# Tiles 0 and 1 multiply w_in in float32, and all steps stand in another order

## The chip, the cores and the metric

The kernel runs on one NeuronCore of one Trainium2 chip. The metric is the device time of one execution in microseconds, from start to end of the program on that core. Its engines work side by side, each through its own queue of instructions in program order: PE (TensorE, matmuls, with PEld for the weight loads that run beside them), DVE (VectorE), ACT (ScalarE), POOL (GpSimd) and SP, whose queue here issues every DMA.

## The reference

Three layers follow one another on an input of 2 x 768 rows. Cut to what matters:

```
# 1. attention: 8 heads of 64, in chunks of 32 queries
k_full = [8 memory keys, 16 keys before, the chunk's 32, 8 after]
a = softmax(q_c @ k_full.T / 8);   x = a @ v_full        # x: (2, 768, 512)

# 2. a gated layer with a product over the rows of the sequence
h = gelu_tanh(x @ w_in)                                  # w_in: 512 x 1024
u, v = h[..., :512], h[..., 512:]
v_n = (v - mean(v)) / sqrt(var(v) + 1e-6) * g_ln
gated = u * (w_sg @ v_n + b_sg)                          # w_sg: 768 x 768
x = x + gated @ w_out                                    # w_out: 512 x 512

# 3. a gated layer with a convolution of width 3 along the sequence
h = relu(x @ w_in2)                                      # 512 x 1024
out = (h * sigmoid(conv3(h, conv_w))) @ w_out2           # 1024 x 512
```

The weights w_in, w_out, w_in2, w_out2 and conv_w reach the kernel as 64-bit floats.

## The kernel before, in words

**Tiles.** The 1536 rows are 12 tiles of 128 (0 to 5 are batch 0, 6 to 11 batch 1). Layers 2 and 3 also work in four groups of 384 columns (three tiles each).

**Products in halves.** Outside attention, each operand of a product is scaled by a power of two and split into two float16 halves, hi and lo. `mm3` (line 230) makes a product from three float16 matmuls: hi·hi, hi·lo, lo·hi. This needs work before the first matmul. A weight piece is narrowed from 64 to 32 bits (`cn`, three DVE instructions, lines 251 to 254), its largest magnitude is taken (`ca`, ACT, line 239; `wta`, `wtb`, `wtc`, `wtd` bring it across the partitions over PE, DVE, PE, DVE), then the halves are made (`wh`, ACT, line 281; `wl`, DVE, line 289). A tile's x goes the same way: `xa`, `ta`, `tb`, `tc`, `td`, then `xh` and `xl`. The scale is taken out in the step that reads the result, with a factor that `iv` computes.

**Steps of a tile.** Attention of tile i: loads `lq` (queries and keys) and `lv` (values), scores `qk` on PE, maximum `mx` and difference `sb` on DVE, `ex` on ACT, transposes `pp` on PE, copy `pt` on ACT, `pv` on PE, `rd` and `xn` on DVE. Then x is transposed (`px`, PE) and copied into the float32 tile `xf` (`xc`, ACT). Then `v.i.k` (four steps, one for each 128 rows of w_in, 512 columns each) and `u.i.j` (four steps of 128 output columns, all four k inside) form the two parts of x @ w_in, `vg` and `ug` apply gelu on ACT, and `vb`, `nr`, `np`, `nn`, `vn`, `vh`, `vl` normalize v and halve it.

**Later stages.** `m.g.j.n` is the product with w_sg, `o` the one with w_out, `i` the one with w_in2, `p` the one with w_out2. Between them stand steps of DVE and ACT and, for each group, a scale chain as above (`ga` to `gd`, `ya` to `yd`, `za` to `zd`). `pe` copies results out of PSUM and `st` stores them.

**Order.** The string `ORDER` (line 42) lists all steps in one sequence, and `run` (line 794) emits each in turn. Each engine works through its own part of that sequence in order. Waits between engines come from data and from reuse of buffers alone. A name after `@` is the PSUM slot (M0 to M3 of one bank, D0 and D1 of two) or the row buffer (R0 to R2) that a step opens. The slot's earlier user must have been read out first.

**Fillers.** `W.n` (`warm`, line 222) is n matmuls of zeros with 512 columns. They compute nothing. `ORDER` holds 74 of them, in the steps `W.12`, `W.7`, `W.6`, `W.19`, `W.4`, `W.11`, `W.3`, `W.12`, all of them before `pv.2`.

**Loads.** All DMAs stand in the SP queue, in the order of the string. It begins `lq.0 lq.2 lq.1 lv.2 lv.1 lv.0`, then the four pieces of the v half of w_in (`lw.v.0` and so on), then `lq.5 lq.3 lq.4`, `lw.u.0 lw.u.1`. A load into a buffer that is still read waits on the queue, and what stands behind it waits too: three buffers each for `lq` and `lv`.

Of the kernel before, what the change touches and what calls it, by code (L numbers as in the profile page):

```python
# [44 lines left out]
ta.1 lq.6 wtd.v ca.u.0 mx.3 lg wh.v.0 iv.v.0 sb.3 wh.v.1 wl.v.0 W.11@M0 qk.5@D1 lc ex.3 wl.v.1 wh.v.3 xl.0 W.3@M0
pp.3@M1 wh.v.2 mx.5 ls.2 v.0.0@M0 pt.3 tb.1 sb.5 tc.1 v.0.1 td.1 ex.5 wl.v.3 qk.4@D1 xh.1 lq.8 iv.v.1 pv.3@D0 wl.v.2
mx.4 lq.7 xl.1 sb.4 cn.u.3 ex.4 W.12@M1 pv.2@D1 lv.6 pp.4@M3 lv.5 rd.3 ca.u.3 rd.2 pp.5@M2 xn.3 pt.4 v.0.2 xn.2 xa.3
cn.u.1 px.3@M1 pt.5 xa.2 ta.3 px.2@M3 xc.3 tb.3 ta.2 cn.u.2 ca.s.1 tc.3 v.0.3 v.1.0@M2 xc.2 v.1.1 td.3 tb.2 ca.s.0  # L50
iv.v.3 cwn tc.2 pv.4@D0 td.2 v.1.2 iv.v.2 lv.7 rd.4 xh.3 qk.6@D1 lw.o.1 xn.4 lw.o.2 v.1.3 xh.2 xl.3 lq.9 px.4@M1
# [825 lines left out]
```

## Time and profile before

| | us |
|---|---|
| median of 3 runs (347.4 to 348.97) | 347.87 |
| the profiled execution, its own time | 348.18 |
| span of its trace, first to last instruction | 346.4 |
| PE busy in that span | 326.9 (94%) |
| DVE busy | 250.0 (72%) |
| ACT busy | 216.7 (63%) |
| mean granted clock of TensorE | 0.995 |

The trace is read by stages: the share of busy time of an engine is a mean over stages with different limits. Times within the trace are microseconds from the start of its span. The clock is a fraction of full speed. PE counts as busy also while it multiplies zeros.

### The profile page before, as it was taken

The page shows a single profiled execution, that of the slowest core. Times are in us where ns is not written, and L with a number is a line of the kernel's source. Part 1 is how long each engine was busy: PE and PEld are TensorE (multiplying, and loading weights), DVE is VectorE, ACT ScalarE, POOL GpSimd, SP SyncE. Part 2 cuts the span into 40 slices and gives each one's busy share as a digit, 9 for nine tenths or more (in the row PEclk, how much of TensorE's full clock was granted, in tenths as well). Part 3 has the DMA queues.
Part 4 walks back from the last instruction along what each step waited for, and adds up shares of the span by engine and source line. Part 5 has one row for each costly group of instructions (what it writes and reads, how often), then busy time and mean ns, then how long its engine had stood idle before and what let it go on. Part 6 is the DMA issues. An engine that isn't in the chain of part 4 may idle for free.

```text
span 346.4 us, 8509 instructions
## 1 busy us (share of the span) xinstructions
PE 326.9 (94%) x3638; PEld 196.3 (57%) x3638; DVE 250.0 (72%) x517; ACT 216.7 (63%) x431; POOL 6.6 (2%) x37
## 2 busy tenths in 40 slices
PE   8679798899999899999999999999999999999995
PEld 3435454498766566666676676565555554444442
DVE  2659797999838999999597759997999953670000
ACT  1428398887725959674367738995899735661112
POOL 1000000101000000010010000000000000000000
PEclk9989999999999999999999999999999999999999
DMA  7999949404502450033330000100000001001113
GB/s 292 382 417 406 348 107 339 154 2 131 180 0 65 129 177 5 0 125 123 121 123 2 0 2 1 62 1 0 2 0 2 0 0 63 0 30 62 50 40 122
DMA packets 11909, 35.20 MB, mean 102 GB/s; under 512 B 1760, under 2 KB 1760, under 8 KB 11872
## 3 DMA queue, kind: packets, MB, share of 16 engines
q1 hardware_dynamic: 11872, 34.67, 28.1%
q8 instruction: 28, 0.46, 0.6%
q14 instruction: 9, 0.07, 0.1%
HBM read 31.52 MB, written 3.15 MB: 100 GB/s over the span
## 4 chain that ended last, share of the span: by engine, by line
PE 78%; DVE 9%; ACT 7%; issue 3%; DMA 2%; ACTq 0%; SPq 0%; DVEq 0%
PE up L235 9%; PE warm L226 6%; PE vp L235 4%; PE e0.2_3983 L235 3%; PE e1.2_4078 L235 3%; PE po L477 2%; PE sc L438 2%; DMA raw<-in_w_out_dram 2%; PE o20.2_3975 L235 2%; PE o21.1_4215 L235 1%; PE o21.3_4074 L235 1%; PE o21.0_4084 L235 1%; PE o20.0_3778 L235 1%; PE o21.2_4158 L235 1%; ACT hb L732 1%
## 5 line engine op out<-in xcount | busy, mean ns | idle before, releaser
L235 PEld LDWEIGHTS <-i 128*128 128x128 f16 x384 | 37.1, 98 | 27.0 <-issue 2.2
L235 PEld LDWEIGHTS <-gsp 128*128 128x128 f16 x288 | 28.1, 98 | 32.9 <-issue 0.6
L740 DVE SCALAR_TENSOR_TENSOR cb<-hb,cw,cb 128x768 f32<-128x768 f32 x32 | 32.1, 1012 | 7.7 <-ACT cb L737 7.5
L235 PEld LDWEIGHTS <-vs 128*128 128x128 f16 x288 | 27.4, 98 | 17.5 <-issue 0.8
L235 PE MATMUL up<-xs,win 128*128 128x128 f16 x576 | 36.4, 219 | 0.0
L235 PE MATMUL vp<-win,xs 128*128 128x512 f16 x144 | 36.0, 379 | 0.4 <-DVE scwu L269 0.2
L235 PEld LDWEIGHTS <-win 128*128 128x128 f16 x576 | 33.7, 98 | 4.0 <-DVE win L289 0.2
L235 PEld LDWEIGHTS <-wo 128*128 128x128 f16 x192 | 18.5, 98 | 12.6 <-issue 0.9
L226 PE MATMUL warm<-zero 128*128 128x512 f16 x74 | 21.3, 443 | 1.2 <-DVE zero L202 1.2
L235 PEld LDWEIGHTS <-xs 128*128 128x128 f16 x144 | 13.1, 97 | 14.6 <-issue 3.5
L748 DVE TENSOR_TENSOR gate<-hb,cb 128x768 f32<-128x768 f32 x16 | 15.2, 954 | 4.4 <-ACT cb L745 4.4
L745 ACT ACTIVATE cb<-cb 128x768 f32<-128x768 f32 x16 | 13.4, 840 | 7.1 <-DVE cb L740 6.9
L289 DVE SCALAR_TENSOR_TENSOR gsp<-gate,scz,gsp 128x768 f16<-128x768 f32 x16 | 15.7, 1012 | 2.3 <-ACT gsp L281 2.2
L458 ACT ACTIVATE sring<-sring 128x512 f32<-128x512 f32 x12 | 7.5, 628 | 14.9 <-DVE sring L454 14.7
L281 ACT ACTIVATE gsp<-gate,scz 128x768 f16<-128x768 f32 x16 | 14.2, 930 | 3.0 <-DVE gate L748 1.6
L450 DVE TENSOR_REDUCE mx<-sc 128x8 f32<-128x512 f32 x12 | 8.1, 684 | 9.8 <-PE sc L438 9.8
L737 ACT ACTIVATE cb<-hb,cw 128x768 f32<-128x768 f32 x16 | 14.8, 929 | 0.1
L477 PE MATMUL po<-vw,ptr 64*32 64x65 f32 x768 | 10.6, 225 | 4.3 <-issue 3.9
L239 ACT ACTIVATE gs<-uf 128x384 f16<-128x384 f32 x16 | 8.3, 517 | 10.0 <-DVE uf L635 10.0
L226 PEld LDWEIGHTS <-zero 128*128 128x128 f16 x74 | 7.6, 110 | 11.4 <-issue 5.0
L239 ACT ACTIVATE x2s<-xf 128x384 f16<-128x384 f32 x16 | 8.3, 518 | 8.6 <-DVE xf L676 8.6
L477 PEld LDWEIGHTS po<-vw,ptr 64*32 64x32 f32 x768 | 8.5, 105 | 8.1 <-issue 5.7
(403 smaller groups left out, 686.1 us busy)
## 6 DMA issues: line engine op xcount, KB each, us to landing
qk<-in_qk_dram SPq DMA_DIRECT2D x12, 624.0 KB, 6.2
vw<-in_vw_dram SPq DMA_DIRECT2D x12, 520.0 KB, 6.8
raw<-in_w_out_dram SPq DMA_DIRECT2D x12, 512.0 KB, 3.5
raw<-in_w_in_dram SPq DMA_DIRECT2D x8, 512.0 KB, 3.5
ts<-in_w_sgt_dram SPq DMA_DIRECT2D x3, 768.0 KB, 11.0
...
```

The source lines that it names most:

```text
L226: self.nc.tensor.matmul(ps, self.zero[:, :P], self.zero, start=True, stop=True)
L235: self.nc.tensor.matmul(ps, a, b, start=first and i == 0, stop=last and i == n - 1)
L239: self.nc.scalar.activation(room, src, AF.Abs, scale=2.0 ** (1 - EXP_TOP), accum_out=acc)
L281: self.nc.scalar.activation(hi, src, AF.Copy, scale=sc[:, 0:1])
L289: self.nc.vector.scalar_tensor_tensor(out=lo, in0=src, scalar=sc[:, 0:1], in1=hi, op0=ALU.mult, op1=ALU.subtract)
L450: self.nc.vector.tensor_reduce(out=m, in_=self.scv(i), axis=AX.X, op=ALU.max)
L458: self.nc.scalar.activation(self.s(i), self.s(i), AF.Exp, scale=0.125)
L477: self.nc.tensor.matmul(po[c * CH:(c + 1) * CH, par, hp * (D + 1):(hp + 1) * (D + 1)], t[rows, hp, c * CH:(c + 1) * CH], v[rows, c, hp, :] ...
L737: self.nc.scalar.activation(self.c(f), self.h(f)[:, 1:S + 1], AF.Copy, scale=self.cw[:, f, 1:2])
L740: self.nc.vector.scalar_tensor_tensor(out=self.c(f), in0=self.h(f)[:, 2 * side:S + 2 * side], scalar=self.cw[:, f, 2 * side:2 * side + 1], ...
L745: self.nc.scalar.activation(self.c(f), self.c(f), AF.Sigmoid)
L748: self.nc.vector.tensor_tensor(out=self.gate(b, f), in0=self.h(f)[:, 1:S + 1], in1=self.c(f), op=ALU.mult)
```

## The change

It does four things.

1. For tiles 0 and 1 (`PLAIN`), `v.i.k` becomes one float32 matmul of 512 columns, of `xf` with the narrowed float32 piece of w_in, in place of three float16 ones. `u.i.j` becomes four float32 matmuls of 128 columns in place of twelve.
2. For these two tiles the steps `xa`, `ta`, `tb`, `tc`, `td`, `xh`, `xl`, `iv.v` and `iv.u` are gone, and gelu reads the result with a factor of 1.
3. The fillers go from 74 to 38: `W.0.8`, `W.1.16`, `W.3.5`, `W.2.3`, `W.4.3`, `W.5.3` (the first number is a name, the second the count).
4. All other steps stay the same in kind and number, but the whole string, with the loads in it, is in another order. The loads now begin `lw.v.0 lq.0 lw.v.2 lw.v.3 lq.1 lw.v.1 lv.0`.

The start of the new string, up to the first steps of tile 4, and the edits of the code:

```diff
+PLAIN = (0, 1)
+lw.v.0 lq.0 lw.v.2 lw.v.3 lq.1 lw.v.1 cn.v.0 ca.v.0 lv.0 W.0.8@M0 qk.0@D0 mx.0 W.1.16@M1 cn.v.2 ca.v.2 sb.0 qk.1@D1
+lw.u.0 lv.1 lq.2 lw.u.1 W.3.5@M2 ex.0 cn.v.3 ca.v.3 lw.u.2 pp.0@M3 lq.3 pt.0 lv.2 W.2.3@M0 pv.0@D0 lq.4 cn.v.1
+ca.v.1 ls.1 wta.v@M1 W.4.3@M2 mx.1 sb.1 rd.0 xn.0 px.0@M3 xc.0 wtb.v wtc.v W.5.3@M0 ex.1 v.0.0@M2 wtd.v wh.v.0
+wh.v.2 cn.u.0 ca.u.0 cn.u.1 pp.1@M1 pt.1 wh.v.1 wl.v.0 ca.u.1 v.0.1 v.0.2 pv.1@D1 wh.v.3 wl.v.2 rd.1 xn.1 qk.2@D0
+v.0.3 qk.3@D1 mx.2 sb.2 ls.0 px.1@M3 vg.0@R0 lw.u.3 lg ex.2 mx.3 qk.4@D0 wl.v.1 xc.1 pp.2@M0 lv.3 sb.3 lb cn.u.2
+lv.4 lc lq.5 v.1.0@M1 ex.3 pp.3@M2 mx.4 sb.4 pt.2 pv.2@D1 rd.2 xn.2 ca.s.1 v.1.1 v.1.2 ex.4 pp.4@M3 pt.3 xa.2 ca.u.2
+cn.u.3 pv.3@D0 rd.3 ta.2 tb.2 pt.4 px.2@M0 u.1.0@M2 lw.o.0 tc.2 xn.3 ca.u.3 wl.v.3 ls.2 wta.u@M3 wtb.u xc.2 v.1.3
+lv.6 wtc.u lq.6 xa.3 ta.3 td.2 iv.v.2 xh.2 u.1.1 lv.5 ca.s.0 wtd.u wh.u.2 tb.3 vb.0 wh.u.1 tc.3 xl.2 td.3 pv.4@D1
+rd.4 cwn px.3@M0 xc.3 u.1.2 qk.5@D0 lq.8 lw.o.2 v.2.0@M3 ca.s.2 xn.4 px.4@M0 xc.4 v.2.1 wl.u.1 xh.3 u.1.3 lq.7
+wta.s@M0 mx.5 sb.5 wl.u.2 v.2.2 wtb.s wtc.s xl.3 wtd.s iv.v.3 wh.u.3 xa.4 lw.o.1 qk.6@D0 wl.u.3 v.2.3 iv.u.2 ta.4
+tb.4 mx.6 ex.5 ug.1 v.3.0@M0 v.3.1 sb.6 tc.4 td.4 v.3.2 wh.u.0 wl.u.0 pp.5@M2 vg.1@R1 vb.1 xh.4 pt.5 lv.7 v.3.3
+vg.2@R2 wh.s.0 u.2.0@M1 qk.7@D0 pv.5@D1 xl.4 v.4.0@M2 vb.2 rd.5 xn.5 iv.v.4 u.2.1 wh.s.5 wh.s.1 nr.0 np.0 v.4.1 xa.5
...
     def v(self, i, k):
         b, ts = self.ts(i)
+        if i in PLAIN:
+            self.nc.tensor.matmul(self.bank(f"vp{i}"), self.xf(b)[:, k, ts], self.f32("v", k)[:, 0],
+                                  start=k == 0, stop=k == KD - 1)
+            return
...
     def u(self, i, j):
         b, ts = self.ts(i)
+        if i in PLAIN:
+            for k in range(KD):
+                self.nc.tensor.matmul(self.bank(f"up{i}")[:, j * P:(j + 1) * P],
+                                      self.f32("u", k)[:, 0, j * P:(j + 1) * P], self.xf(b)[:, k, ts],
+                                      start=k == 0, stop=k == KD - 1)
+            return
...
     def vg(self, i):
-        self.nc.scalar.activation(self.v_(i), self.bank(f"vp{i}"), AF.Gelu_apprx_tanh, scale=self.inv(f"x{i}", "v"))
+        self.nc.scalar.activation(self.v_(i), self.bank(f"vp{i}"), AF.Gelu_apprx_tanh, scale=self.inv(f"x{i}", "v") if i not in PLAIN else 1.0)
```

`ug` takes the same edit as `vg`, and `warm` a second argument for its name. In the new string the four `u.0` steps come later, among those of tile 3.

## Rows read from the trace of the kernel before

**Rows 1.** Stretches: length; PE, PEld, DVE, ACT, POOL busy us; clock; DMA share; GB/s.

```profile
0.00:70.00 70.00, 58.02 (x1179) 32.06 (x1180) 50.16 (x129) 40.95 (x80) 2.92 (x30) 0.98 0.82 302
70.00:340.00 270.00, 266.48 (x2452) 163.35 (x2451) 199.81 (x389) 174.14 (x347) 3.73 (x7) 1.00 0.15 49
```

**Rows 2.** The same view in other stretches, of the first 40 us and of 33.5 to 64.2.

```profile
0.00:10.00 10.00, 8.81 (x211) 4.23 (x211) 2.78 (x5) 2.25 (x3) 1.70 (x29) 1.00 0.82 308
10.00:20.00 10.00, 5.11 (x155) 3.53 (x149) 6.04 (x12) 4.00 (x9) 0.00 (x0) 0.98 1.01 385
20.00:30.00 10.00, 9.62 (x105) 4.72 (x104) 6.76 (x17) 4.28 (x12) 0.00 (x0) 0.85 1.03 411
30.00:40.00 10.00, 8.12 (x221) 4.63 (x220) 8.37 (x19) 5.48 (x10) 0.00 (x0) 1.00 1.04 383
...
33.50:64.20 30.70, 25.43 (x614) 15.04 (x612) 25.41 (x70) 22.59 (x45) 0.23 (x1) 1.00 0.70 242
```

**Rows 3.** The chain that ended last: start us, length us, what it stood on.

```profile
15.37 3.92 issue
19.61 5.87 PE warm L226 x19
...
81.86 1.34 PE up L235 x24
```

**Rows 4.** Timeline: start us, us, engine, line, operation; brackets: idle before, what ended it.

```profile
6.19 1.32 PEld L438 LDWEIGHTS sc<-qk 64*32 64x32 f32 x128 [0.61 <-DMA qk<-in_qk_dram]
...
14.15 0.43 DVE L251 TENSOR_SCALAR tv<-rawv 128x512 int32<-128x512 int32 x1 [2.61 <-DMA rawv<-in_w_in_dram]
...
19.12 0.43 DVE L251 TENSOR_SCALAR tv<-rawv 128x512 int32<-128x512 int32 x1 [0.99 <-DMA rawv<-in_w_in_dram]
...
27.59 0.60 PE L527 MATMUL px<-ident,xx 128*128 128x128 f32 x4
...
33.48 0.81 PE L235 MATMUL vp<-win,xs 128*128 128x512 f16 x3
...
64.21 0.81 PE L235 MATMUL vp<-win,xs 128*128 128x512 f16 x3
```

**Rows 5.** Groups by line and shape, PE: busy us, mean ns of one, idle before.

```profile
L226 PE MATMUL warm<-zero 128*128 128x512 f16 x74 | 21.3, 443 | 1.2 <-DVE zero L202 1.2
L235 PEld LDWEIGHTS <-xs 128*128 128x128 f16 x144 | 13.1, 97 | 14.6 <-issue 3.5 <-DVE xs L289 0.2
L477 PE MATMUL po<-vw,ptr 64*32 64x65 f32 x768 | 10.6, 225 | 4.3 <-issue 3.9 <-ACT ptr L470 0.2
L438 PE MATMUL sc<-qk 64*32 64x64 f32 x768 | 10.3, 224 | 2.0 <-issue 1.8
L527 PE MATMUL px<-ident,xx 128*128 128x128 f32 x48 | 7.3, 277 | 0.9 <-DVE scwo L269 0.8
L527 PEld LDWEIGHTS px<-ident,xx 128*128 128x128 f32 x48 | 5.5, 141 | 2.6 <-ACT ptr L470 1.0 <-PE warm L226 0.6 <-ACT xf L531 0.2
```

**Rows 6.** The same view, DVE: steps that are removed, and those ahead of the first product.

```profile
L289 DVE SCALAR_TENSOR_TENSOR xs<-xf,scx,xs 128x512 f16<-128x512 f32 x12 | 8.7, 742 | 0.0
L450 DVE TENSOR_REDUCE mx<-sc 128x8 f32<-128x512 f32 x12 | 8.1, 684 | 9.8 <-PE sc L438 9.8
L254 DVE SCALAR_TENSOR_TENSOR tv<-rawv,tv 128x512 int32<-128x512 int32 x4 | 2.8, 692 | 0.1
L251 DVE TENSOR_SCALAR tv<-rawv 128x512 int32<-128x512 int32 x4 | 1.7, 423 | 3.6 <-DMA rawv<-in_w_in_dram 3.6
```

**Rows 7.** The same view, ACT: table loads and the steps that are removed.

```profile
L281 ACT ACTIVATE xs<-xf,scx 128x512 f16<-128x512 f32 x12 | 8.4, 714 | 0.4 <-DVE scx L269 0.4
L239 ACT ACTIVATE xs<-xx 128x512 f16<-128x512 f32 x12 | 7.6, 630 | 2.1 <-DVE xx L496 2.1
L458 ACT ACT_TABLE_LOAD x3 | 3.8, 1283 | 0.8 <-PEq L866 0.7
```

**Rows 8.** A wait of the SP queue: waiting line, waited for, total us, times, longest us.

```profile
SPq L300 <- PE po L477: 38.3, 7, 22.5
```

More of the change, by code (lines that the diff above doesn't have):

```diff
@@ L47 @@
[L47 to L51, printed above, removed]
@@ new lines @@
+o.1.0.0@M0 xl.7 o.1.2.1 td.8 iv.v.8 pv.10@D0 o.1.0.1 os.1.2 o.1.1.0@M1 gl.0.0 o.0.1.0@M2 iv.u.8 os.1.0 oa.1.0
+o.1.1.1 oa.1.2 gl.0.1 o.0.1.1 iv.v.7 rd.9 xn.9 xa.9 o.1.3.0@M0 os.1.1 oa.1.1 o.0.0.0@M1 rd.10 xn.10 xa.10 os.0.1
+o.1.3.1 o.0.0.1 ta.9 oa.0.1 os.1.3 tb.9 o.0.2.0@M2 xh.8 xl.8 vb.6 o.0.3.0@M0 os.0.0 oa.0.0 o.0.2.1 os.0.2 ta.10
+oa.1.3 o.0.3.1 px.9@M1 oa.0.2 ya.1@M2 os.0.3 tc.9 u.6.2 tb.10 tc.10 xc.9 td.9 iv.u.9 xh.9 px.10@M0 oa.0.3 xc.10 yb.1
+yc.1 yd.1 yh.1.1 yh.1.0 td.10 xh.10 iv.v.10 v.7.0@M1 xl.9 qk.11@D1 ya.0@M2 yb.0 v.8.0@M0 yc.0 yd.0 mx.11 sb.11 v.7.1
@@ new lines @@
+v.11.0@M0 ca.i0.1 v.10.2 v.11.1 vl.6 wta.i0@M1 v.10.3 wtb.i0 wtc.i0 vg.9@R2 vl.8 vg.10@R0 u.11.0@M2 wtd.i0 yi.i0.1
+yi.i0.0 wh.i0.3 wh.i0.0 wh.i0.1 wh.i0.2 v.11.2 m.2.1.0@M1 vb.9 u.11.1 m.3.0.0@M3 v.11.3 vg.11@R1 vb.10 wl.i0.1
+wl.i0.0 i.0.3.0.0@D1 i.0.0.0.0@D0 lw.i1.0 cn.i1.0 lw.i1.3 ca.i1.0 wl.i0.2 vb.11 nr.3 np.3 m.2.0.0@M0 wl.i0.3
+i.0.0.1.0 i.0.0.0.1 hr.0.0.0 nn.3 vn.9 vh.9 i.0.3.1.0 cn.i1.3 i.0.0.1.1 vl.9 u.11.2 vn.10 vn.11 lw.p0.2 m.2.0.1
+hr.0.0.1 i.0.1.0.0@D0 hc.0.0 ca.i1.1 iv.u.11 cn.i1.2 u.11.3 vh.10 i.0.1.1.0 cn.p0.0 i.0.1.0.1 i.0.1.1.1 vh.11 vl.11
@@ new lines @@
+lw.p1.2 ca.p0.0 mg.3.0 ma.3.0 m.3.1.2 i.0.5.0.0@D1 ms.3.2@R1 mg.3.2 ms.2.3@R2 ms.3.1@R0 ca.p0.3 i.0.2.1.1 hg.0.3
+hm.0.3 wh.i1.2 i.0.5.1.0 ca.p0.1 yi.i1.0 m.3.3.1 mg.2.3 ma.2.3 wl.i1.2 cn.p1.2 i.0.5.1.1 i.0.5.0.1 hr.0.2.1 m.3.3.2
+ga.2@M0 hr.0.5.1 cn.p1.0 lw.p1.3 hr.0.5.0 hc.0.5 i.0.4.0.0@D1 cn.p1.1 gb.2 ca.p0.2 mg.3.1 ma.3.2 i.0.2.0.1 gc.2
+i.0.4.1.0 i.0.4.0.1 ca.p1.0 hr.0.2.0 hc.0.2 gd.2 gh.2.0 gh.2.1 i.0.6.0.0@D0 ms.3.3@R1 ma.3.1 hs.0.5.0 i.0.4.1.1
+i.0.6.1.0 hs.0.5.1 mg.3.3 ma.3.3 gl.2.0 o.2.1.0@M1 hg.0.5 hs.0.2.0 hs.0.2.1 ga.3@M2 o.2.2.0@M0 o.2.0.0@M3 gb.3
@@ new lines @@
+p.0.2.0@M3 p.0.0.0@M1 p.0.3.0@M0 hs.1.1.1 wh.p1.2 wh.p0.1 hg.1.1 hs.1.2.0 hs.1.2.1 zh.0.1 zl.0.1 i.1.4.1.0 i.1.4.0.1
+hm.1.1 wh.p1.1 wl.p1.1 hg.1.2 i.1.4.1.1 hr.1.3.0 hr.1.3.1 p.0.0.1 p.0.1.0@M2 p.0.4.0@D1 p.0.2.1 p.0.5.0 hm.1.2
+hr.1.4.0 hr.1.4.1 i.1.5.0.0@D0 zh.0.3 zl.0.3 zh.0.4 zl.0.4 p.0.5.1 zh.0.2 zl.0.2 hc.1.3 zh.0.6 zl.0.6 p.0.1.1
+wh.p1.3 wh.p0.2 wh.p0.3 p.0.4.1 wl.p0.1 i.1.5.1.0 wl.p1.2 wl.p0.2 p.0.3.1 i.1.5.1.1 p.0.4.2 zh.0.7 p.0.0.2 hs.1.3.0
+hs.1.3.1 p.0.3.2 hc.1.4 wl.p1.3 zl.0.7 p.0.4.3 p.0.3.3 p.0.5.2 p.0.4.4 i.1.5.0.1 p.0.5.3 p.0.4.5 p.0.3.4 hg.1.3
@@ L121 @@
+p.1.2.4 p.1.3.4 p.1.2.5 p.1.3.5 p.1.2.6 pe.1.1@R0 st.1.1 p.1.3.6 p.1.2.7 pe.1.2@R2 st.1.2 p.1.3.7 pe.1.3@R1 st.1.3
 """
@@ L220, in consts, with warm @@
             nc.gpsimd.memset(self.red[n], 2.0 ** -120)
-    def warm(self, n):
-        ps = self.ps.tile([P, 512], F32, tag=self.slot, name="warm")
+    def warm(self, i, n):
+        ps = self.ps.tile([P, 512], F32, tag=self.slot, name=f"warm{i}")
         for _ in range(n):
```

119 lines of the change are left out of this document (45 added, 74 removed).

## The prediction

> **What bounds the kernel now.** I read the stretches of the span first. After 70 us PE is busy for 266.5 of 270 us [rows 1], and at full rate: 24 matmuls of 128 columns take 1.34 us [rows 3], 56 ns each. There only fewer matmuls would help. In the first 70 us PE is busy for 58.0, but 21.3 of these are the 74 fillers [rows 5], all issued before the first product of tile 1. Real work in the first 70 us is 36.7; 33.3 us are idle or zeros. That is what a better start could win, at most.
>
> Next the chain that ended last, in that stretch: it stands on fillers and on a wait of 3.92 us [rows 3]. So PE waits for something. The timeline says for what: the first scores start when a DMA lands at 6.19, DVE begins to narrow w_in at 14.15, again behind a DMA, and the first product starts at 33.48 [rows 4]. Up to 40 us the DMAs move 383 to 411 GB/s once they run [rows 2]. Before the first product stand three tiles of attention on the load queue and, on DVE, ACT and PE, the scales and halves of w_in and x. From 33.5 to 64.2 PE and DVE are both 83% busy and ACT 74% [rows 2]: a region in which the engines wait on one another, and which prepares u, w_sg and the later tiles.
>
> **The change, part by part.**
>
> *Float32 products.* The nearest rows are the transposes px: four of 128 float32 columns end in 0.60 us [rows 4], and one alone lasts 277 ns [rows 5], so they follow each other every (600-277)/3 = 108 ns, against 56 for float16. Scores and pv, which are float32 matmuls, show 768 instructions for 12 x 32 calls [rows 5], so a float32 matmul is two instructions. Per 128 columns that makes 2 x 108 = 216 ns, against 3 x 56 = 168 for the three float16 ones. v: 8 matmuls of four such widths, 6.9 us for 5.2. u: 32 matmuls, 6.9 for 5.4. Sum +3.2 us of PE. Upper bound: a float32 load of 128 columns lasts 141 ns against 97 [rows 5]; if all 80 stood open, 11.3 us more, so +14.5. The lower bound is the 108 ns once per matmul, -3.6, which the two instructions speak against. I take +3.2: px runs at its rate with the same loads hidden.
>
> The Trainium skill ("TensorE: Matmul & The Clock Gate", section "Weight-path perf modes — Fast Weight Load (FWL) and DoubleRow") says that the fast weight load is off for FP32, which speaks against this change. The 141 against 97 ns agree in direction, though whether loads then stand in the open no row here shows for a real float32 product. By its figure for a plain load, an estimate of 107 ns for 128 columns, all 80 in the open would make +11.8 instead of +3.2 us.
>
> *What leaves.* For two tiles, xl (0.74) and the small tb, td and iv on DVE, 1.5 us and somewhat over; xh (0.71) and xa (0.63) on ACT, 2.7 us [rows 6, 7]; ta and tc, a few tenths of PE. All of it counts only in the start, where these engines set the pace. Against it, the new string switches ACT between exp and gelu more often: counted from both strings, 13 table loads for 11, +2.6 us at 1.28 [rows 7]. They lie on ACT in the stretch that matters, and I carry them there.
>
> *Loads.* What moves earlier or later is DMA issue in SP's queue too. Bytes from the shapes: lq 0.64 MB, lv 0.53, a piece of w_in 0.52. Now 1.28 MB are in at 6.2 us, 4.04 at 14.15, 5.61 at 19.1 [rows 4]. The same line through the new order gives lq.0 (1.16 MB) at 6, lw.v.1 (3.37) at 12.2, lv.0 (3.9) at 13.8, lw.u.3 (10.55) at 31, lv.4 (12.0) at 35. The last two at 0.4 MB per us [rows 2].
>
> *The first product.* DVE narrows three pieces and does mx.0 and sb.0 while loads arrive. After lw.v.1 at 12.2 it still has cn.v.1 (0.42 + 2 x 0.69 = 1.8), mx.1 and sb.1 (0.68 each), rd.0 and xn.0 (1.0): done at 16.4 [rows 6]. px (0.6) and xc (0.6) with their hand-overs put v.0.0 at 18, instead of 33.5: 15 us earlier. The fillers fall from 74 to 38, but they only ever filled.
>
> *From there to the first step of tile 4.* I compare the stretch from v.0.0 to the first product of tile 5 now (33.5 to 64.2) with xn.0 to v.4.0 after. Steps counted from the strings, each at its mean: DVE 28.8 us now, 33.3 after (eight wl for two, ten mx and sb for five, four cn for five, three xl for five); ACT 25.6 now, 34.7 after (nine wh for none, two more ex, a ug, three table loads for one). Now 28.8 and 25.6 show as 25.4 and 22.6 busy [rows 2], a factor of 0.88, so 29.4 and 30.6 after. At the 83% that the fuller engine reaches now, DVE needs 35.4 us from 16.4, ACT 36.9 from 17.9: v.4.0 starts between 51.8 and 54.8. I take 53.3.
>
> *The end.* Real PE work now: 326.9 busy less 21.3 = 305.6; after, 308.8. Done before v.5.0 at 64.2 now: nine qk at 0.86, six pv at 0.88, seven pp and six px at 0.6, sixteen v at 0.65 and small ones [rows 4, 5], together 32.0; left 273.6. The span has 346.4 - 64.2 = 282.2 us for it, so 8.6 are idle (the stores of the end among them). Done before v.4.0 after: eight qk, six pv, six pp, five px, 6.9 of float32 v, 3.5 of float32 u, eight v, one u, small ones: 35.6; left 273.2. With the same 8.6 idle the span is 53.3 + 273.2 + 8.6 = 335.1. The profiled execution lies 1.8 above its span and 0.3 above the median: 336.6, say **336.5 us**.
>
> Later stages I leave as they are. Summed along the strings in the same way, the work that stands ahead of m.0.2.2 is now 79 us on DVE and 59 on PE, after the change 76 and 67; ahead of i.0.0.0.0 it is 148 and 127 now, 142 and 145 after. DVE has less of a lag to make up, so PE should run full there. The tightest place is the last third of m, where m.0.2.2 waits for vl.4, which stands behind mx.10 on DVE, which waits for qk.10 on PE.
>
> **The rivals.**
>
> *More is won (326 to 331).* If DVE and ACT run at 97% in the start instead of 83%, v.4.0 starts at 16.4 + 30.3 to 17.9 + 31.5, about 48, and the time is 331; with the later idle halved, 327. For it: the new order has more steps ready at a time. Against: no stretch of the start shows both engines so full.
>
> *Part is given back (341.5 to 346).* Open weight loads cost up to 11.3 us, of which u.0 and the late half lie where PE is the bound: 5 to 6 more. Or a load is late: SP takes its steps in order, and now has waited 22.5 us behind one pv [rows 8]. In the new string lq.7 stands behind lq.8, which waits for qk.5; its 17.5 MB are in at about 49, and qk.7 is due at 51. Each us beyond stands in front of v.4.0. Either gives 342 to 346.
>
> *No change (346.1 to 349.6).* Both together, about 11 us, and the end is where it was.
>
> *Slower (350 to 365).* The clock. After the idle of 3.92 us the granted clock of 20 to 30 us is 0.85 [rows 2, 3], so part of it ran at 1.2 GHz, while fillers covered the rest of the start. With half the fillers, small gaps could hold PE at 1.2 GHz from 18 to 53 us. PE's 32 us of work there would need up to 64, so v.4.0 would come up to 29 us late. The point from which it is a loss: 14 us late, a mean clock of about 0.65 in that stretch. Against: from 30 to 40 us PE had gaps of 19% at 1.00 [rows 2].
>
> The Trainium skill (the same page, section "Part 1: The HAM clock gate (the "warmup" mystery)") says that the slow clock is the default and activity lifts it, so fewer fillers speak for this rival. The drop to 0.85 behind the idle stretch agrees.
>
> **How the numbers follow.** Forecast, 331 to 341: 0.52. More won: 0.13. Part given back, 341 to 346.1: 0.18. No change: 0.07. Slower: 0.10. A measurement of this kernel tells about 0.5% from no change, 346.1 to 349.6. Faster is then 0.83, same 0.07, slower 0.10. The range from 327 to 346.5 leaves out slower, most of no change and the edge below.
>
> **What the profile will show.** If the steps are right: first float32 product at 17 to 20 us; v.4.0 at 52 to 55; 0.86 us for each float32 v or u step; fillers about 11 us; clock above 0.95 in every stretch from 10 us on; PE over 98% busy from 60 us on. I am wrong if v.4.0 is in time and PE idles over 9 us behind it, if PE's real work exceeds 312 us, or if the clock stays low after 20 us.

## The result, and the profile after

| | before | after |
|---|---|---|
| median, us | 347.63 (347.37 to 348.97) | 335.83 (333.63 to 337.3) |
| ratio, 95% interval | | 0.965 (0.959 to 0.971) |
| profiled execution, us | 348.18 | 336.14 |
| span, us | 346.4 | 334.3 |
| PE busy, us | 326.9 | 319.8 |
| fillers, us (count) | 21.3 (74) | 11.9 (38) |
| DVE, ACT busy, us | 250.0, 216.7 | 250.5, 215.7 |
| mean granted clock | 0.995 | 0.995 |

The kernel is 11.8 us faster, and 335.83 stands 0.7 us beside the forecast of 336.5. One execution among all runs, of e2 (350.44 us), was in a slower state of the chip and is left out of its median. The stretches of the changed kernel come first; columns as in [rows 1] and [rows 2], and the last line is of the kernel before.

```profile
0.00:70.00 70.00, 62.00 (x1296) 42.20 (x1297) 54.30 (x127) 48.79 (x84) 3.18 (x30) 0.98 0.79 284
70.00:334.30 264.30, 257.76 (x2266) 154.10 (x2263) 196.24 (x379) 166.94 (x344) 3.94 (x7) 1.00 0.17 58
...
0.00:10.00 10.00, 6.16 (x76) 2.57 (x77) 3.38 (x7) 2.01 (x3) 1.70 (x29) 1.00 0.80 249
20.00:30.00 10.00, 7.31 (x235) 4.24 (x235) 9.72 (x18) 9.24 (x16) 0.00 (x0) 1.00 1.03 403
30.00:40.00 10.00, 9.80 (x199) 6.83 (x199) 6.22 (x14) 6.71 (x14) 0.00 (x0) 0.83 0.90 324
...
19.76:55.94 36.18, 32.58 (x834) 22.42 (x834) 29.71 (x73) 31.57 (x55) 0.00 (x0) 0.95 0.92 335
55.94:334.30 278.36, 271.82 (x2490) 166.61 (x2484) 209.19 (x409) 178.35 (x361) 5.42 (x8) 1.00 0.17 59
```
```profile
70.00:346.40 276.40, 268.87 (x2462) 164.23 (x2460) 199.81 (x389) 175.79 (x351) 3.73 (x7) 1.00 0.15 51
```

The first two lines answer to [rows 1], and they hold the whole balance. All fillers lie in the first 70 us, so PE's real work there is 62.0 - 11.9 = 50.1 us, where it was 36.7: 13.4 more. Real work in the whole span is 319.8 - 11.9 = 307.9, where it was 305.6: 2.3 more. Behind 70 us 6.5 are idle (264.3 - 257.8) for 7.5 before (276.4 - 268.9). 13.4 - 2.3 + 1.0 = 12.1, which is the difference of the spans. The gain was made in the start and nowhere given back.

The chain that ended last, pieces of the start (start us, length us, what it stood on):

```profile
3.25 10.79 DMA rawv<-in_w_in_dram
...
19.76 1.13 PE vp L547 x2
...
27.35 2.85 issue
...
31.68 1.71 PE vp L547 x2
...
38.92 0.89 PE up L558 x8
...
39.95 0.86 PE vp L547 x2
...
46.88 7.46 DMA qk<-in_qk_dram
...
57.44 0.65 PE vp L236 x3
...
58.52 0.67 PE up L236 x12
```

Read from the top: the last piece of w_in's v half lands at 14.04, the first product stands at 19.76 (33.48 in [rows 4]). A float32 step of v takes 0.86 us and one of u 0.89, against 0.65 and 0.67 for the steps in halves lower down. v.1.0 at 31.68 takes 1.71, twice as long, in the stretch with the clock at 0.83. Ahead of it stands a piece of 2.85 us named "issue", of which more below. v.4.0 follows at 55.94. Just ahead of it PE waits once more, for the load lq.7:

```profile
54.47 0.85 PE L439 MATMUL sc<-qk 64*32 64x64 f32 x64 [0.71 <-DMA qk<-in_qk_dram]
```

The groups by line and shape that answer to [rows 5] (busy us, mean ns of one, idle before):

```profile
L547 PE MATMUL vp<-tv,xf 128*128 128x512 f32 x16 | 9.0, 670 | 0.0
L558 PE MATMUL up<-xf,tu 128*128 128x128 f32 x64 | 8.7, 278 | 0.0
...
L558 PEld LDWEIGHTS up<-xf,tu 128*128 128x128 f32 x64 | 7.9, 192 | 0.4
L547 PEld LDWEIGHTS vp<-tv,xf 128*128 128x128 f32 x16 | 2.8, 207 | 1.6 <-issue 1.0 <-ACT xf L532 0.5
```

8 and 32 float32 matmuls in the code are 16 and 64 here, two instructions each. A float32 weight load lasts 192 to 207 ns, twice the 97 of [rows 5], but PE is never idle ahead of a float32 product (0.0 in both lines), and a step of u with eight loads takes no longer than a step of v with two (0.89 and 0.86 us): the loads are hidden.

### The profile page after: what moved, and what is told of

Its sections match the earlier page's. It is cut to its first block, busy times and chain, and to the rows that moved or that the text cites. A ratio compares the mean times of both kernels' runs of the same rounds, so it can differ in the third digit from the quotient of the medians.

```text
span 334.3 us, 8332 instructions
## 1 busy us (share of the span) xinstructions
PE 319.8 (96%) x3558; PEld 196.3 (59%) x3558; DVE 250.5 (75%) x505; ACT 215.7 (65%) x427; POOL 7.1 (2%) x37
## 4 chain that ended last, share of the span: by engine, by line
PE 87%; DMA 5%; DVE 3%; ACT 2%; issue 1%; SPq 1%; ACTq 0%
PE up L236 8%; PE vp L236 6%; DMA rawv<-in_w_in_dram 3%; PE e1.2_3976 L236 3%; PE e0.2_3672 L236 3%; PE po L478 3%; PE vp L547 3%; DMA qk<-in_qk_dram 2%; PE sc L439 2%; PE up L558 2%; PE px L528 2%; PE pp L464 2%; PE o20.2_3621 L236 2%; PE o21.3_4068 L236 2%; PE o21.0_3993 L236 2%; PE o21.1_3984 L236 2%
## 5 line engine op out<-in xcount | busy, mean ns | idle before, releaser
L236 PE MATMUL up<-xs,win 128*128 128x128 f16 x480 | 32.2, 219 | 0.0
L236 PEld LDWEIGHTS <-win 128*128 128x128 f16 x480 | 29.2, 98 | 4.7
L236 PE MATMUL vp<-win,xs 128*128 128x512 f16 x120 | 31.3, 379 | 0.0
L236 PEld LDWEIGHTS <-wo 128*128 128x128 f16 x192 | 18.6, 98 | 12.2
L756 ACT ACTIVATE cb<-cb 128x768 f32<-128x768 f32 x16 | 13.4, 836 | 11.9 <-DVE cb L751 11.9
L439 PE MATMUL sc<-qk 64*32 64x64 f32 x768 | 10.9, 231 | 6.3 <-DMA qk<-in_qk_dram 3.4
L439 PEld LDWEIGHTS sc<-qk 64*32 64x32 f32 x768 | 8.7, 109 | 10.4 <-issue 5.7
L236 PEld LDWEIGHTS <-xs 128*128 128x128 f16 x120 | 10.5, 98 | 7.1
L236 PE MATMUL e1.2_3976<-wp,gsp 128*128 128x512 f16 x48 | 12.5, 379 | 1.7 <-ACT o1.5_4103 L800 1.7
L227 PE MATMUL warm<-zero 128*128 128x512 f16 x38 | 11.9, 462 | 1.2 <-DVE zero L203 1.2
L236 PE MATMUL e0.2_3672<-wp,gsp 128*128 128x512 f16 x48 | 12.3, 379 | 0.0
L240 ACT ACTIVATE xs<-xx 128x512 f16<-128x512 f32 x10 | 6.3, 628 | 7.4 <-DVE xx L497 7.4
```

The costliest lines, as they stand in the source:

```text
L227: self.nc.tensor.matmul(ps, self.zero[:, :P], self.zero, start=True, stop=True)
L236: self.nc.tensor.matmul(ps, a, b, start=first and i == 0, stop=last and i == n - 1)
L240: self.nc.scalar.activation(room, src, AF.Abs, scale=2.0 ** (1 - EXP_TOP), accum_out=acc)
L439: self.nc.tensor.matmul(sc[c * CH:(c + 1) * CH, par, hp * 64:(hp + 1) * 64], q[rows, hp, c * CH:(c + 1) * CH], k[rows, hp, KSTEP * c:KSTEP ...
L756: self.nc.scalar.activation(self.c(f), self.c(f), AF.Sigmoid)
```

## The experiments

Each run stands beside runs of the kernel before on the same chip; the ratio is to those.

| run | what it is | median us | ratio, 95% interval |
|---|---|---|---|
| changed kernel | | 335.83 | 0.965 (0.959 to 0.971) |
| e1 | old order, float32 products | 354.49 | 1.019 (1.018 to 1.021) |
| e5 | e1, one load and its scan later | 351.97 | 1.012 (1.009 to 1.015) |
| e6 | e1, v.0 and v.1 early | 356.39 | 1.025 (1.022 to 1.028) |
| e2 | new order, halves for all tiles | 343.97 | 0.989 (0.987 to 0.990) |
| e3 | changed kernel, no fillers | 340.63 | 0.980 (0.978 to 0.982) |
| e4 | changed kernel, w_sg not loaded | 337.16 | 0.969 (0.966 to 0.972) |
| e8 | w_sg and the u half of w_in not loaded | 332.31 | 0.956 (0.953 to 0.959) |
| e7 | changed kernel, qk.4 later | 335.92 | 0.964 (0.961 to 0.967) |
| e9 | changed kernel, lq.7 earlier | 336.93 | 0.969 (0.968 to 0.970) |
| e10 | changed kernel, 12 small matmuls more | 334.12 | 0.961 (0.960 to 0.963) |
| e11 | e7 and e9, one gelu later | 334.43 | 0.963 (0.961 to 0.965) |
| e12 | e10 and e11 | 334.87 | 0.965 (0.963 to 0.968) |

### Order and float32 products, one without the other

**e1, float32 products in the old order.** The string of before without the steps that part 2 of the change removes, with the new `v`, `u`, `vg`, `ug`. The load ls.2 had to go behind lv.7: it fills the room of the narrowed pieces of w_in, which float32 products hold until v.1.1.

```diff
+PLAIN = (0, 1)
-... mx.5 ls.2 v.0.0@M0 pt.3 ...
+... mx.5 v.0.0@M0 pt.3 ...
-... v.1.2 iv.v.2 lv.7 rd.4 ...
+... v.1.2 iv.v.2 lv.7 ls.2 rd.4 ...
```

> The old order with all 74 fillers, but v and u of tiles 0 and 1 as float32 products and their scale and half steps gone; the one load ls.2 stands later, since its buffer still holds the float32 w_in. Theory (the gain is the early start that the new order gives, and float32 is only what allows it): v.0.0 stays at about 33 us, because transposes and scores of the old order stand in front of it, and the time stays within 344 to 350 us. Rival (the float32 products and the fewer steps of DVE and ACT are the gain by themselves): 335 to 341 us in the old order as well.

354.49 us: slower than before by 1.9%, and outside of both expectations. A timeline shows part of the cause: first a row of ACT, then one of PE.

```profile
57.03 1.48 ACT L241 ACTIVATE wsg<-ts 128x1536 f16<-128x1536 f32 x1 [5.82 <-DMA ts<-in_w_sgt_dram]
```
```profile
59.13 1.44 PE L237 MATMUL vp<-win,xs 128*128 128x512 f16 x3 [3.39 <-ACT xf L533]
```

ACT stands 5.82 us before ca.s.2, the scan of the late load; behind it on ACT waits the copy xc.4, and behind that copy PE, 3.39 us.

**e5, e1 with that load and its scan out of the way.**

```diff
-... lv.7 ls.2 rd.4 ... px.4@M1 ca.s.2 lw.o.0 xl.2 ... ca.o.1 iv.v.5 ...
+... lv.7 rd.4 ... px.4@M1 lw.o.0 ls.2 xl.2 ... ca.o.1 ca.s.2 iv.v.5 ...
```

> The old order with float32 products for tiles 0 and 1, as in the run before it, but the load ls.2 and its scan ca.s.2 stand later (ls.2 behind lw.o.0, ca.s.2 behind ca.o.1), because there ACT stood 5.8 us before ca.s.2 and PE 3.4 us behind the copy that follows it. Theory (the float32 pieces of w_in are held longer, so ls.2, which reuses their room, came late and blocked ACT; the products themselves cost little): 347 to 350.5 us, and PE busy over 8 us between 50 and 60 us. Rival (float32 products are dear in the old order in themselves): 352 to 356 us.

351.97, between the two. The blocked ACT was worth 2.5 us; 4.4 remain by the medians, 3.5 in the profiled executions (351.71 and 348.18), where they can be found:

```profile
34.48 1.88 PE L548 MATMUL vp<-tv,xf 128*128 128x512 f32 x4
```
```profile
66.15 5.34 PE L237 MATMUL vp<-win,xs 128*128 128x512 f16 x24 [1.42 <-ACT ptr L472]
```

The first product stands at 34.48, no earlier than before (33.48), because in the old string it follows qk.5 and the fillers. The 1.0 us arises ahead of any float32 product: the granted clock from 20 to 30 us is 0.76 for 0.85 before, and the 19 fillers there take 6.83 us for 5.92. The products of tiles 4 and 5 begin at 66.15 instead of 64.21, another 0.9 us later, and what is left takes 349.9 - 66.15 = 283.8 us instead of 282.2; all eight float32 steps of u lie there, 8 x 0.22 = 1.8 us dearer. Where nothing starts earlier, the steps saved bring nothing and the longer products are paid.

**e6, e1 with v.0, v.1 and their gelu moved up,** in place of 18 fillers; ls.2 goes back to its old place.

```diff
-... W.59.4@M1 wta.v@M2 px.1@M3 wtb.v ... xc.1 wtc.v lq.6 ...
+... wta.v@M2 px.1@M3 v.0.0@M0 v.0.1 v.0.2 v.0.3 wtb.v ... xc.1 wtc.v v.1.0@M1 v.1.1 v.1.2 v.1.3 lq.6 ...
```

> The old order with float32 products, and of all steps only these moved: v.0 and v.1 with their gelu directly behind the copies of x for tiles 0 and 1, in place of 18 fillers. Theory (what float32 brings is that real products can start some 12 us earlier; the rest of the order matters less): v.0.0 at 28 to 30 us, time 340 to 346 us. Rival (the rest of the old order, with qk.3 to qk.5 and their DVE work ahead of tiles 2 and 3, sets the end of the start): v.0.0 early, yet 346.5 to 352 us.

356.39, the slowest of all, although the first products are early:

```profile
27.59 3.60 PE L548 MATMUL vp<-tv,xf 128*128 128x512 f32 x8
...
41.22 0.86 PE L479 MATMUL po<-vw,ptr 64*32 64x65 f32 x64 [2.16 <-ACT ptr L472]
42.01 4.45 PE L228 MATMUL warm<-zero 128*128 128x512 f16 x12
```

Both theories missed. In front of the next steps PE now waits for ACT (2.16 us at once) and DVE (2.07), and 12 fillers that I had left where they were take 4.45 us ahead of pv.2; the clock is 0.83 from 40 to 50 us and 0.66 from 50 to 60. So in this string early products don't help. Whether they would without those fillers, and what the rest of the old order costs by itself, the run can't tell.

**e2, the new order with halves for all tiles.** The removed steps stand again in the new string, u.1 moves behind vg.4 because its halves come later, and the steps of v.0, vg.0 and wl.v.3 are shifted to fit.

```diff
-PLAIN = (0, 1)
+PLAIN = ()
-... px.0@M3 xc.0 wtb.v wtc.v W.5.3@M0 ex.1 v.0.0@M2 wtd.v wh.v.0 ...
+... px.0@M3 xc.0 xa.0 ta.0 tb.0 wtb.v wtc.v tc.0 W.5.3@M0 ex.1 wtd.v td.0 iv.v.0 xh.0 wh.v.0 ...
-... wl.v.0 ca.u.1 v.0.1 v.0.2 pv.1@D1 ...
+... wl.v.0 xl.0 ca.u.1 v.0.0@M2 pv.1@D1 ...
```

> The new order with its 38 fillers, but tiles 0 and 1 in float16 halves: xa to xl of both tiles go back in, v.0 and v.1 stand where their halves are ready, u.1 stands behind gelu of tile 4. Theory (the order carries most, float32 the rest): the chain xa to xl puts v.0.0 some 4 us later, and 3.6 us of u.1 leave the start for the stretch where PE is the bound, less 3.2 us of dearer products: 338 to 344 us. Rival (float32 is the whole gain): 346 us or more, no better than the kernel before.

343.97, at the upper edge of the expected range; the order without float32 products is 4.1 us faster than the kernel before beside it (348.07). The new order with them is 8.1 us faster still. Rows of PE in the start, then of DVE, and the stretch from 20 to 30 us:

```profile
22.88 0.63 PE L237 MATMUL vp<-win,xs 128*128 128x512 f16 x1
26.04 0.38 PE L237 MATMUL vp<-win,xs 128*128 128x512 f16 x1 [2.52 <-DVE win L291]
```
```profile
24.63 0.69 DVE L256 SCALAR_TENSOR_TENSOR tu<-rawu,tu 128x512 int32<-128x512 int32 x1
25.24 0.74 DVE L291 SCALAR_TENSOR_TENSOR win<-tv,scwv,win 128x512 f16<-128x512 f32 x1
```
```profile
20.00:30.00 10.00, 6.54 (x144) 3.46 (x143) 7.67 (x19) 6.08 (x13) 0.00 (x0) 0.71 1.03 399
```

The scale of x and the hi half put the first matmul of v.0.0 at 22.88, 3.1 us behind the float32 one. It then waits 2.52 us for the lo half on DVE, which in this string stands behind cn.u.0 and cn.u.1 (3.6 us, the `tu` row is their end). From 20 to 30 us DVE and ACT are busy for 7.7 and 6.1 of 10 us, less than in the changed kernel (9.7 and 9.2), PE for 6.5, and the clock is 0.71: what is lost here are hand-overs between engines and the place of the lo half in DVE's order, and not that DVE and ACT are full throughout. The float32 product needs neither step.

Put together: float32 products cost 4.4 us in the old order (e5), of which about 1 arises ahead of them, and bring 8.1 in the new one. Neither half of the change alone makes the gain. My placing of the removed steps in e2 is one of many (wl.v.0 could stand ahead of cn.u.0), so 8.1 is an upper value for what they cost there.

### Fillers and the clock

**e3, the changed kernel without its 38 fillers.**

```diff
-... lv.0 W.0.8@M0 qk.0@D0 mx.0 W.1.16@M1 cn.v.2 ...
+... lv.0 qk.0@D0 mx.0 cn.v.2 ...
```

> The changed kernel without its 38 fillers. Theory (they fill waits and keep the clock up, and PE is not the bound before 30 us): 335 to 339 us, with a granted clock below 1 in one or two stretches of the first 40 us. Rival of the prediction (the clock decides the start): PE at 1.2 GHz up to 40 us or beyond, v.4.0 at 62 us or later, 343 us or more.

340.63: 4.8 us more than with them, between the two. v.0.0 begins at 19.63, as with them (19.76), so the fillers did not hold it up. But its steps take twice as long:

```profile
19.63 2.07 PE L547 MATMUL vp<-tv,xf 128*128 128x512 f32 x2 [0.67 <-ACT xf L532]
...
29.27 0.81 PE L439 MATMUL sc<-qk 64*32 64x64 f32 x58 [1.12 <-issue]
...
31.38 0.33 PE L464 MATMUL pp<-ident,sring 128*128 128x128 f32 x1
35.58 0.80 PE L464 MATMUL pp<-ident,sring 128*128 128x128 f32 x3 [3.87 <-issue]
```

2.07 us for what takes 1.13 with fillers, as v.1.0 takes twice as long where the clock is low in the changed kernel. The view of stretches still shows a granted clock of 1.00 there:

```profile
20.00:30.00 10.00, 8.88 (x204) 4.66 (x203) 6.53 (x12) 7.68 (x14) 0.00 (x0) 1.00 1.03 403
```

That column counts time without a record of the clock as full, and the first record in this trace begins at 24.71 us (10.53 in the changed kernel). That PE ran at 1.2 GHz ahead of it is read from the doubled durations alone: pv.1, behind v.0.2, begins at 25.34 instead of 22.97, 2.4 us late. Two idle times within a step add to this: 1.12 us in qk.3, where the changed kernel has none, and 3.87 in pp.2 for its 2.85. v.4.0 comes at 59.71 instead of 55.94.

### Loads

**e4, without the load of w_sg;** a GpSimd memset fills its tiles, so that the results are other ones.

```diff
-        self.nc.sync.dma_start(dst, self.blocks(self.src["s"])[:, 2 * j:2 * j + 2])
+        self.nc.gpsimd.memset(dst, 0.01)
```

> The changed kernel, but the three loads of w_sg (2.36 MB of the first 14) are left out and GpSimd fills the tiles with a constant. Theory (in the start PE waits on the transfers, for data and also in the middle of a step, 2.85 us inside qk.4 at 27.4 us): that wait falls below 1 us, the granted clock stays at 1.00 from 30 to 40 us, v.4.0 starts by 53 us, and the time is 329 to 333 us. Rival (DVE and ACT set the pace of the start anyway): 334.5 to 337 us, v.4.0 at 55 to 57 us.

337.16: 2.36 MB less bring nothing that can be measured. The clock stays at 1.00 from 30 to 40 us as the theory has it, but the wait in qk.4 is still 1.51 us, v.4.0 comes at 55.16 (not by 53), and the time is at the upper end of the rival's: the theory fell.

**e8, also without the u half of w_in,** by the same edit in `load_lw`.

> The changed kernel without the loads of w_sg and of the u half of w_in; a GpSimd memset fills their tiles instead (4.5 MB less in the first 36 us, the results are then other ones). Theory (PE's idle times in the middle of a step are instruction fetches that queue behind full DMA engines): the DMA engines fall below 0.7 of their time between 24 and 32 us, no idle time over 0.8 us inside a step there, clock above 0.97 from 20 to 40 us, 329 to 333.5 us. Rival (the idle times do not hang on the DMA load): one of 1.5 us or more remains between 20 and 32 us, 334 to 337.5 us.

332.31: 3.5 us less than the changed kernel (and 3.6 less than e7, 335.92, run on the same chip). The time is the theory's, and the clock stays at 1.00 from 20 to 40 us; its mechanism is only half right. PE still stands in the middle of qk.2, 1.68 us, and of qk.4, 0.96 us. The first of the two:

```profile
22.90 0.56 PE L442 MATMUL sc<-qk 64*32 64x64 f32 x32
25.14 0.45 PE L442 MATMUL sc<-qk 64*32 64x64 f32 x30 [1.68 <-issue]
```

The same in the view of stretches (columns as above):

```profile
23.40:25.20 1.80, 0.12 (x12) 0.06 (x13) 1.24 (x4) 1.60 (x2) 0.00 (x0) 1.00 0.58 119
```

PE stands there with the DMA engines busy for 0.58 of the time, so full DMA engines are no condition for it. In e4 the two idle times are 2.21 and 1.51 us long.

### The idle time in the middle of a step

In the changed kernel PE stands 2.85 us inside qk.4, between two matmuls of one step, and no semaphore (the signal by which one engine releases another) ends the wait. Two rows of PE's timeline in the changed kernel:

```profile
26.91 0.43 PE L439 MATMUL sc<-qk 64*32 64x64 f32 x27
30.20 0.63 PE L439 MATMUL sc<-qk 64*32 64x64 f32 x37 [2.85 <-issue]
```

And what the queue that brings instructions did from 27 to 28 us there (packets, MB, share of the engines):

```profile
q8 instruction: 1, 0.02, 6.8%
```

One packet falls into the idle time; it starts at 27.66. The 3.92 us of before [rows 3] are of the same kind; PE's timeline there:

```profile
13.93 1.45 PE L477 MATMUL po<-vw,ptr 64*32 64x65 f32 x120 [0.24 <-ACT ptr L470]
19.29 0.32 PE L477 MATMUL po<-vw,ptr 64*32 64x65 f32 x8 [3.92 <-issue]
```

They stand 8 matmuls ahead of the end of a pv, as they do in e1, e5 and e6, and an instruction packet falls into them too (from 16.5 to 17.5 us). e3 has one from 32.5 to 33.5, inside its 3.87 us. That led to the idea that PE runs out of instructions.

**e7, qk.4 behind v.1.0.**

```diff
-... ex.2 mx.3 qk.4@D0 wl.v.1 ... lq.5 v.1.0@M1 ex.3 ...
+... ex.2 mx.3 wl.v.1 ... lq.5 v.1.0@M1 qk.4@D0 ex.3 ...
```

> The changed kernel with one step moved: the scores qk.4 stand behind v.1.0 instead of ahead of pp.2. In the changed kernel PE stands 2.85 us in the middle of qk.4, without a wait on anybody, and pp.2 and v.1.0 behind it were ready at about 29 us. Theory (PE runs out of instructions in a run of short ones, pv, qk, qk, qk; with qk.4 behind the long float32 products the next instructions are there): no idle time over 1 us inside a step between 20 and 40 us, v.4.0 at 53 to 55 us, 332.5 to 335 us. Rival (the wait comes at the same count of instructions, whatever they are): it only moves, 335 to 338 us.

335.92, no different from the changed kernel, and the rival was right: idle times of 1.98 and 1.27 us stand in other steps.

```profile
25.52 0.65 PE L439 MATMUL sc<-qk 64*32 64x64 f32 x30 [1.98 <-issue]
...
38.44 0.80 PE L478 MATMUL po<-vw,ptr 64*32 64x65 f32 x56 [1.27 <-issue]
```

**e9, lq.7 ahead of lq.8 in SP's queue,** with PE's instructions untouched.

```diff
-... qk.5@D0 lq.8 lw.o.2 ... u.1.3 lq.7 wta.s@M0 ...
+... qk.5@D0 lq.7 lq.8 lw.o.2 ... u.1.3 wta.s@M0 ...
```

> The changed kernel with one load moved: lq.7 ahead of lq.8 in the SP queue, so that it no longer stands behind the wait of lq.8 for qk.5. PE's instructions stay the same ones. Theory (the 0.71 us that PE waits before qk.7 is the late load, as the prediction's rival had it, only smaller): no wait before qk.7, v.4.0 up to 0.7 us earlier, 334.8 to 335.7 us, hardly more than can be measured. Rival (qk.7 would have waited for something else as well): 335.7 to 337 us. On the idle time in the middle of a step: if it comes at a count of instructions, it stands again in qk.2 behind about 32 or in qk.4 behind about 27 records of 64.

336.93, at the upper end of the rival's range. The wait before qk.7 is gone, so the load was its cause, but PE stood 2.22 us in qk.2 and 3.16 us in qk.4, 2.5 us more than in the changed kernel, and v.4.0 came at 57.00. Both stand where the expectation put them: the second again behind 27 records.

**e10, 12 matmuls of 64 columns more in W.0.**

```diff
+        for _ in range(12 if i == 0 else 0):
+            self.nc.tensor.matmul(ps[:, :64], self.zero[:, :P], self.zero[:, :64], start=True, stop=True)
```

> The changed kernel with 12 small matmuls of zeros (64 columns) more in W.0, where PE waits for the first load anyway. In three kernels the idle time in the middle of a step stood behind record 32 of 64 in qk.2 and behind record 27 in qk.4; every record there is a weight load and a matmul. Theory (PE's instructions come in blocks of a fixed count, and PE runs dry at the end of a block): 24 instructions more in front move these points 12 records forward, to about 20 in qk.2 and 15 in qk.4. Rival (the points belong to the data or to these steps): they stay at 32 and 27. Time by both 335 to 338 us.

```profile
26.23 0.34 PE L441 MATMUL sc<-qk 64*32 64x64 f32 x15
28.96 0.96 PE L441 MATMUL sc<-qk 64*32 64x64 f32 x49 [2.39 <-issue]
```

The idle time moved from record 27 to record 15, 12 forward, as the theory has it; at the earlier place, in qk.2, none is seen, as in the changed kernel. 334.12 us, a little below the expected 335.

**e11, with lq.7 and qk.4 moved as above, and the gelu of tile 0 later,** so that ACT's two table loads no longer stand before ex.2.

```diff
-... px.1@M3 vg.0@R0 lw.u.3 lg ex.2 ... v.1.2 ex.4 pp.4@M3 ...
+... px.1@M3 lw.u.3 lg ex.2 ... v.1.2 ex.4 vg.0@R0 pp.4@M0 ...
```

> The changed kernel with lq.7 ahead of lq.8, qk.4 behind v.1.0, and vg.0 (with its two table loads on ACT) behind ex.4 instead of ahead of ex.2; PSUM slots M0 and M3 change places from pp.3 on to make room. With qk.4 later PE waited 0.98 us before pp.2 for ex.2, which stood behind 1.28 + 0.60 + 1.28 us of vg.0 and table loads on ACT. Theory (these 3.2 us of ACT lie on the path between the stall and v.1): pp.2 at 26.5 to 28.5 us, v.4.0 at 53 to 54.5 us, 332 to 334.5 us. Rival (the table loads only meet the next step of ACT, ca.u.2 and pt.4, and the gain is given back by 40 us): 335 to 338 us.

```profile
26.66 0.66 PE L464 MATMUL pp<-ident,sring 128*128 128x128 f32 x4 [0.33 <-ACT sring L459]
...
28.20 0.41 PE L439 MATMUL sc<-qk 64*32 64x64 f32 x21
30.85 0.68 PE L439 MATMUL sc<-qk 64*32 64x64 f32 x43 [2.24 <-issue]
```

334.43: the time and pp.2 at 26.66 are the theory's, v.4.0 at 55.62 is not. pp.2 and v.1.0 now run ahead of the idle time, but it still comes.

**e12, both edits.**

> Both edits that came out fastest together: the order of e11 (lq.7 earlier, qk.4 behind v.1.0, vg.0 behind ex.4) and the 12 small matmuls more of e10. Theory (what is left of the stretch from 20 to 34 us is the supply of PE with instructions, and its idle time is what the times differ by): one idle time inside qk.4, 12 records ahead of e11's, at about record 9; 332 to 335 us, so no gain on e10 beyond 1 us. Rival (the gains of the two edits add up, as they lie on ACT and on PE): 331 to 333 us, and v.4.0 before 54 us.

```profile
28.50 0.32 PE L441 MATMUL sc<-qk 64*32 64x64 f32 x9
29.23 0.78 PE L441 MATMUL sc<-qk 64*32 64x64 f32 x55 [0.42 <-issue]
...
35.47 0.66 PE L466 MATMUL pp<-ident,sring 128*128 128x128 f32 x4 [2.16 <-ACT xs L242]
```
```profile
31.50 0.63 ACT L461 ACTIVATE sring<-sring 128x512 f32<-128x512 f32 x1 [0.78 <-DVE sring L457]
```

334.87, in the theory's range. The idle time stands behind record 9 as foretold, and was only 0.42 us long, but it is not the only one. PE stands 2.16 us ahead of pp.4. The profile puts that down to ACT, yet ex.4, which makes what pp.4 reads, ends at 32.13 (the ACT row), 3.3 us before pp.4 begins, and the place is 55 + 4 + 64 + 4 = 127 records behind the last one: by the count that follows it is a wait of the same kind. e10 to e12 have medians 1.0 to 1.7 us below the changed kernel's, with overlapping intervals: no version is shown to beat it.

**What follows.** A record is a weight load and a matmul, two instructions. The places can be counted:

| run | idle time stands behind | counted from the changed kernel |
|---|---|---|
| changed kernel | qk.4, 27 | |
| e4, e8, e9 | qk.2, 34 (the first two are shown apart), and qk.4, 27 | same instructions, same places |
| e3 | qk.3, 6, and pp.2, 1 | 38 fillers less: 34 + 38 is 6 into qk.3, 27 + 38 is 1 into pp.2 |
| e10 | qk.4, 15 | 27 - 12 |
| e11 | qk.4, 21 | pp.2 (4) and v.1.0 (2) come first: 27 - 6 |
| e12 | qk.4, 9, and ahead of pp.4 | 21 - 12, and 127 records on |
| e7 | qk.2, 34, and pv.3, 8 | 127 records after place 21 of qk.4 |

From 34 in qk.2 to 27 in qk.4 there are 30 + 2 + 64 + 4 + 27 = 127 records, 254 instructions. Counted along the strings from PE's first matmul, the idle times of this kind stand at 222, 349, 475, 602 and 730 records, within two, in every kernel here, the one before included (222, 349 and 603): 127 apart, whatever step is there. That PE can run dry at such a place is shown.

How long it stands is not fixed. In qk.4, for the same instructions, the traces say what the length hangs on: PE goes on 2.3 to 2.5 us after the packet of the instruction queue starts, and the packet starts sooner or later after PE has begun the 127 records ahead of the place.

| run | 127 records begin, us | packet starts | PE goes on | idle |
|---|---|---|---|---|
| changed kernel | 23.93 | 27.66 | 30.20 | 2.85 |
| e9 | 25.68 | 29.68 | 32.08 | 3.16 |
| e4 | 26.40 | 28.82 | 31.16 | 1.51 |
| e8 | 25.14 | 27.06 | 29.35 | 0.96 |

In all other idle times of this kind the packet starts 2.2 to 2.6 us before PE goes on, too (2.26 in the kernel before, 2.64 in e3, 2.58 ahead of pp.4 in e12). PE runs through such 127 records in 3.2 us (e9, from 25.68 to 28.92), so even a packet that starts 1.9 us into them comes late. Where it starts early enough nothing is seen: in the changed kernel one starts at 20.11, and PE passes 34 in qk.2 at 23.93 without a wait. The packet starts 1.9 us in with the fewest loads (e8), 2.4 in e4 and 3.7 to 4.0 with all of them. That it queues behind the loads fits these four, but is not shown.

The Trainium skill ("Runtime: NRT & Kernel Launch", section "Instruction fetch mechanics") says that an engine's instructions are refilled in blocks of 16 KiB, 256 instructions, and that the cost of crossing a boundary is mostly hidden. The count agrees with the 254 here. The cost does not: it was visible, up to 3.92 us [rows 3], and the measurement decides.

## Why the prediction was right, step by step

**What bounds the start.** The frame held: the win came from 33.3 us of idle time and zeros in the first 70 us. One reading was wrong. I took the 3.92 us in the chain [rows 3] for a wait of PE for data. They are PE without instructions, in the middle of a pv, 127 records behind another such idle time. The changed kernel has its own of 2.85 us.

**Float32 products.** Predicted 0.86 us for a step of v or u and +3.2 us in all. Measured 0.86 and 0.89, against 0.65 and 0.67: 8 x 0.21 + 8 x 0.22 = 3.4 for the steps; PE's real work grew by 2.3. The choice between the bounds was right, and for its reason: loads are longer than I thought (192 to 207 ns against 141) and still hidden. The Trainium skill ("TensorE: Matmul & The Clock Gate", section "Weight-path perf modes — Fast Weight Load (FWL) and DoubleRow") says that the fast weight load is off for FP32. The trace agrees, with 192 to 207 ns against 97, but the estimate of +11.8 us fell: the loads are not in the open.

**What leaves.** 13 table loads were counted and 13 are there (5, 5 and three single ones). "They only ever filled" was wrong of the fillers: without the 38 that are left the kernel is 4.8 us slower (e3), and 2.4 of it stand where PE's first products take twice as long.

**Loads and the first product.** This term was mis-sized. lw.v.1 was due at 12.2, by the bytes of before; it landed at 14.04, as the first 10 us moved 249 GB/s and not 308 [rows 2] (13.3 to 13.6 in e7 to e12, at 261 to 270). From there DVE's steps took 4.3 us to xn.0's end at 18.32, for 4.2 summed. So v.0.0 came at 19.76 instead of 18 (18.9 to 19.2 in e7 to e12). The new string asks for w_in first, and every run of it moves less in the first 10 us than the runs of the old one (249 to 270 GB/s for 308 to 318); why, was not tried.

**From there to tile 4.** Predicted busy 29.4 on DVE and 30.6 on ACT; measured from v.0.0 to v.4.0 29.7 and 31.6 (on DVE 30.5 from xn.0's end). The fuller one reaches 87% and not 83%. v.4.0 was forecast at 53.3 and came at 55.94: 1.8 of the 2.6 us are the late first product. For the other 0.9 there are the idle time of 2.85 us, the slow clock behind it and the 0.71 us for lq.7, less what the better 87% gives back; they are not measured apart.

**The end.** Forecast were 273.2 us of work and 8.6 idle behind v.4.0, measured 271.8 and 6.5: 3.4 less. So the forecast of 335.1 for a span of 334.3 is closer than its parts: a start that came 2.6 later than forecast and an end 3.4 shorter nearly cancel. That it came this near is luck; that the gain lies in the start is not. The tightest place was harmless: from 60 to 200 us PE is busy all the time.

```profile
60.00:200.00 140.00, 140.00 (x1750) 96.46 (x1747) 122.86 (x271) 94.61 (x190) 3.94 (x7) 1.00 0.27 91
```

**What the profile was to show.** First product between 17 and 20: yes. v.4.0 at 52 to 55: no, by 0.9. Fillers about 11 us: 11.9. Clock above 0.95 from 10 us on: no, 0.83 from 30 to 40. PE over 98% from 60 us on: 97.6% (267.8 of 274.3).

**The rivals.** "Part is given back" was there in small: qk.7 waited 0.71 us for lq.7, issued at 46.88 behind lq.8 as described; e9 takes that wait away. "Slower" was not near: even without any filler (e3), with the first products at half speed, the kernel is 2% faster than before. "More is won" asked for DVE and ACT at 97% in the start; they reach 82% and 87%, and no run comes under 331, not even e8 (332.31) with 4.5 MB less to load. What the prediction didn't ask is which half of the change does it; e2 and e5 answer that neither does alone.
